# Moving the denominator and the spreads of batch 1 one slot earlier in a fused linear attention and feed-forward kernel

## The chip, the cores and the metric

One core of a Trainium2 chip. The metric is the device time of one execution in microseconds (us), as the median of several runs. The profile belongs to one further execution, and its span runs from the first to the last instruction.

## The reference

Linear attention with phi(x) = elu(x) + 1 over 8 batches, 8 heads, 576 positions and a head size of 64, then two matmuls with g = h − tanh(h) between them. The calls are cut to what matters:

```python
q_p, k_p = phi(q), phi(k)
kv  = einsum('bhsd,bhse->bhde', k_p, v)
z   = sum(k_p, axis=2)
num = einsum('bhsd,bhde->bhse', q_p, kv)
den = einsum('bhsd,bhd->bhs', q_p, z)[..., None] + 1e-6
x   = (num / den), heads put side by side      # 4608 x 512
h   = x @ w_in                                 # 512 -> 2048, "layer 1"
g   = h - tanh(h)
out = g @ w_out                                # 2048 -> 512, "layer 2"
```

## The kernel before

The 4608 rows are worked in nine chunks of 512. Layer 1 and layer 2 of a chunk are dense matmuls on TensorE. The attention for the next batch is cut into pieces that are hung between these matmuls. Layer 2 of a chunk has 16 slots of four matmuls each; `s2[n]` holds what is issued behind the four matmuls of slot n. Instructions are issued in program order on each engine, so moving a piece to another slot changes the order on several engines at once. In chunk 0, the attention of batch 1 is placed so (cut):

```python
side = Banks([4, 5, 6, 7])                 # PSUM banks, used in turn
...
s2[7].append(lambda: (a_qT_pe(1, 0, side), a_kv(1, side), a_qT_pe(1, 1, side)))
s2[8].append(lambda: b0_scale_rest(side))
s2[9].append(lambda: (a_den(1, side), num1(), a_split(1)))
s2[11].append(lambda: spread1(0))
...
s2[11].append(lambda: (exp2(qs, q_t, qp_t, "qp", 0), rest2(qs[0])))
s2[12].append(lambda: exp2(qs, q_t, qp_t, "qp", 1))
s2[13].append(lambda: (spread1(1), exp2(ks, k_t, kp_t, "kp", 0), rest2(qs[1]), a_qT_dma(2)))
s2[14].append(lambda: rest2(ks[0]))
```

- `a_qT_pe` transposes phi(q) on TensorE; ScalarE and VectorE copy the result out of PSUM (the tile `ps_all`, eight banks, which every matmul here writes).
- `a_kv` makes kv on TensorE; VectorE masks it into `kz`.
- `a_den` makes the denominator on TensorE. VectorE then adds 1e-6 and takes the reciprocal.
- `num1` makes five pieces of the numerator, which ScalarE copies to SBUF (where most other tiles lie).
- `a_split` cuts 1/den into three bf16 parts on VectorE, the last step giving `w`.
- `spread1` spreads `w` over the partitions with eight matmuls into banks 4 to 7. VectorE then multiplies two parts of the numerator by it: the "scales", which give xT, the input of layer 1 of chunk 1.
- `exp2` and `rest2` are phi of batch 2, exp on ScalarE and the rest on VectorE.
- The output blocks of layer 2 are evacuated by ScalarE at the ends of slots 12 to 15 (`evac`).

## Time and profile before

| | before |
|---|---|
| median of its first 3 runs | 293.37 us |
| span of the profiled execution | 291.8 us |
| TensorE busy | 285.5 us, 98% |
| VectorE, ScalarE busy | 175.1 us, 139.7 us |
| granted TensorE clock | 1.000 |

In the profile, PE is TensorE's matmuls, PEld its weight loads, DVE is VectorE, ACT is ScalarE. The view that counts here is the chain of work that ended last, in order of time: each piece begins where the one that released it ends. A wait of TensorE should show in it as a piece of another engine or as "issue". The lines stand in the prediction below.

### The profile page before, as it was taken

How to read it: one execution, taken by the hardware profiler on the slowest of the kernel's cores; microseconds unless marked ns; L12 is line 12 of the kernel's file. 1: busy time of each engine (PE TensorE's matmuls, PEld its weight loads, DVE VectorE, ACT ScalarE, POOL GpSimd, SP SyncE). 2: the span in 40 equal slices, each digit the busy share in tenths (PEclk: the TensorE clock that was granted, in tenths of full speed). 3: DMA queues.
4: the chain of work that ended last, by engine and by line, in shares of the span. 5: the costliest groups of instructions: out<-in, count | busy, mean ns of one | idle time of the engine just before them, and what ended most of it. 6: DMA issues, size and time to landing. Idle time of an engine off the chain costs nothing.

```text
span 291.8 us, 4505 instructions
## 1 busy us (share of the span) xinstructions
PE 285.5 (98%) x1803; PEld 134.5 (46%) x1803; DVE 175.1 (60%) x266; ACT 139.7 (48%) x168; POOL 33.7 (12%) x56
## 2 busy tenths in 40 slices
PE   8999999999999999999999999999999999999994
PEld 3544464454454444444454444444544444444443
DVE  4759958987468674776478637865581457106600
ACT  4938548846354733465345534751551155126411
POOL 8674030110030003000300030000000000000000
PEclk9999999999999999999999999999999999999999
DMA  7999999997999768965895579666117310130032
GB/s 105 193 202 212 208 206 215 194 183 149 249 158 161 175 128 137 197 146 121 136 223 123 123 139 197 146 138 139 30 38 165 73 36 0 43 83 19 0 74 72
DMA packets 39093, 38.94 MB, mean 133 GB/s; under 512 B 16352, under 2 KB 33824, under 8 KB 38304
## 3 DMA queue, kind: packets, MB, share of 16 engines
q0 software_dynamic: 17568, 18.35, 39.0%
q1 hardware_dynamic: 21344, 20.17, 30.9%
q8 instruction: 14, 0.23, 0.3%
q10 hardware_dynamic: 160, 0.13, 0.1%
q14 instruction: 7, 0.06, 0.1%
HBM read 43.91 MB, written 9.55 MB: 183 GB/s over the span
## 4 chain that ended last, share of the span: by engine, by line
PE 85%; DMA 11%; POOL 2%; issue 1%; DVE 0%; POOLq 0%
PE ps_all L387 39%; PE ps_all L366 38%; DMA v<-in_v_dram 6%; DMA w_in_sb<-in_moe_w_in_dram 3%; PE ps_all L199 2%; DMA kraw<-in_k_dram 2%; PE ps_all L317 2%; PE ps_all L618 1%; PE ps_all L276 1%; POOL v L419 1%; PE ps_all L177 1%; POOL qraw L90 0%; PE ps_all L320 0%; POOL qraw L93 0%; POOL w_out_sb L115 0%
## 5 line engine op out<-in xcount | busy, mean ns | idle before, releaser
L366 PE MATMUL ps_all<-xT,w_in_sb 128*128 128x512 bf16 x574 | 127.6, 379 | 0.0
L387 PE MATMUL ps_all<-w_out_sb,gT 128*128 128x512 bf16 x560 | 127.5, 379 | 0.0
L373 DVE TENSOR_TENSOR gT<-ps_all,th 128x1024 bf16<-128x1024 f32 x64 | 77.9, 1218 | 59.2 <-ACT th L372 59.2
L372 ACT ACTIVATE th<-ps_all 128x1024 f32<-128x1024 f32 x64 | 65.6, 1025 | 57.1 <-PE ps_all L366 46.5
L366 PEld LDWEIGHTS <-w_in_sb 128*128 128x128 bf16 x574 | 55.0, 98 | 66.1 <-issue 0.3
L387 PEld LDWEIGHTS <-gT 128*128 128x128 bf16 x560 | 54.2, 98 | 64.2
L396 ACT COPY osb<-ps_all 128x512 f32<-128x512 f32 (+1 forms) x36 | 20.9, 583 | 71.8 <-PE ps_all L387 52.6
L328 DVE TENSOR_TENSOR xT<-ps_all,rdb 128x512 bf16<-128x512 f32 x24 | 16.5, 691 | 13.7 <-PE ps_all L317 11.2
L134 ACT ACTIVATE e<-qraw 128x1152 bf16<-128x1152 bf16 x16 | 18.5, 1160 | 8.2 <-DMA qraw<-in_q_dram 8.2
L134 ACT ACTIVATE e<-kraw 128x1152 bf16<-128x1152 bf16 x15 | 17.5, 1164 | 0.3 <-DMA kraw<-in_k_dram 0.3
L136 DVE TENSOR_TENSOR qp<-e,r 128x1152 bf16<-128x1152 bf16 x16 | 12.1, 758 | 8.0 <-ACT e L134 7.2
L136 DVE TENSOR_TENSOR kp<-e,r 128x1152 bf16<-128x1152 bf16 x15 | 11.4, 759 | 7.9 <-ACT e L134 6.9
L383 POOL COPY g<-qT 1x1 bf16<-1x1 bf16 x5 | 0.9, 178 | 119.2 <-DMA qT<-qp 119.2
L378 DVE TENSOR_TENSOR gT<-ps_all,th 128x512 bf16<-128x512 f32 x16 | 10.3, 686 | 2.4 <-ACT th L377 1.7
L377 ACT ACTIVATE th<-ps_all 128x512 f32<-128x512 f32 x16 | 9.2, 598 | 4.4 <-PE ps_all L366 3.2
L447 PE MATMUL ps_all<-zero 128*128 128x512 bf16 x29 | 9.2, 480 | 1.2 <-DVE zero L405 1.2
L317 PE MATMUL ps_all<-qT,kz 128*128 128x512 bf16 x28 | 10.1, 379 | 0.0
L135 DVE TENSOR_SCALAR r<-qraw 128x1152 bf16<-128x1152 bf16 x16 | 7.3, 454 | 2.1 <-DMA qraw<-in_q_dram 2.1
L199 PEld LDWEIGHTS <-kp 64*128 64x128 bf16 x216 | 6.4, 94 | 2.5 <-issue 2.1
L285 DVE RECIPROCAL rden<-den 128x144 f32<-128x144 f32 x7 | 7.4, 1053 | 0.2
L199 PE MATMUL ps_all<-vp,kp 64*128 64x136 bf16 x216 | 7.4, 220 | 0.0
L394 DVE COPY osb<-ps_all 128x128 f32<-128x128 f32 x1 | 0.3, 292 | 11.6 <-PE ps_all L618 11.6
(85 smaller groups left out, 123.6 us busy)
## 6 DMA issues: line engine op xcount, KB each, us to landing
out_dram<-osb SPq DMA_DIRECT2D x70, 128.0 KB
rdb<-ds SPq DMA_DIRECT2D x12, 576.0 KB
kraw<-in_k_dram POOLq DMA_DIRECT2D x7, 576.0 KB, 7.1
qraw<-in_q_dram POOLq DMA_DIRECT2D x7, 576.0 KB, 9.1
v<-in_v_dram POOLq DMA_DIRECT2D x7, 576.0 KB, 11.6
w_in_sb<-in_moe_w_in_dram POOLq DMA_DIRECT2D x6, 256.0 KB, 8.7
w_out_sb<-in_moe_w_out_dram POOLq DMA_DIRECT2D x3, 512.0 KB, 14.7
qraw<-in_q_dram POOLq DMA_DIRECT2D x2, 288.0 KB, 4.4
```

The source lines that it names most:

```text
L134: return (lambda: nc.scalar.activation(e, x, AF.Exp), lambda: nc.vector.tensor_scalar(r, x, 0.0, 1.0, ALU.max, ALU.add), lambda: nc.vector ...
L136: lambda: nc.vector.tensor_tensor(y, e, r, ALU.min))
L199: nc.tensor.matmul(ps[hg][:, i, :], kp[r, i, j].rearrange("p h d -> p (h d)"), vp[r, i, j, :], start=(j == 0), stop=(j == J - 1))
L317: nc.tensor.matmul(ps, kz[:, p // 2, p % 2, 0:128], qT[:, p % 2, 0:8, p // 2, :], start=True, stop=True)
L328: nc.vector.tensor_mul(xT[:, p, S * b:S * b + 512].rearrange("p (j t c) -> p j t c", j=8, t=4), ps.rearrange("p j (t c) -> p j t c", t=4), ...
L366: nc.tensor.matmul(h, w_in_sb[:, 2 * (p % 2) + p // 2, fi * 128:(fi + 1) * 128], xT[:, p, c * 512:(c + 1) * 512], start=(n == 0), stop=(n ...
L372: nc.scalar.activation(th, h, AF.Tanh)
L373: nc.vector.tensor_sub(gT[:, fi:fi + 2, :], h, th)
L377: nc.scalar.activation(th, h, AF.Tanh)
L378: nc.vector.tensor_sub(gT[:, fi, :], h, th)
L387: nc.tensor.matmul(o, gT[:, fi, i * 128:(i + 1) * 128], w_out_sb[:, fi, :], start=(fi == 0), stop=(fi == NF - 1))
L396: nc.scalar.copy(osb[:, f0:f1], o[:, f0:f1])
```

## The change

Its intent: start 1/den and num of batch 1 one slot sooner, right behind kv and the transposes, and with it the spreads and scales, so that xT of batch 1 is complete well before layer 1 of chunk 1 needs it.

```diff
-            s2[8].append(lambda: b0_scale_rest(side))
-            s2[9].append(lambda: (a_den(1, side), num1(), a_split(1)))
-            s2[11].append(lambda: spread1(0))
+            s2[8].append(lambda: (b0_scale_rest(side), a_den(1, side), num1(), a_split(1)))
+            s2[10].append(lambda: spread1(0))
...
-            s2[11].append(lambda: (exp2(qs, q_t, qp_t, "qp", 0), rest2(qs[0])))
-            s2[12].append(lambda: exp2(qs, q_t, qp_t, "qp", 1))
-            s2[13].append(lambda: (spread1(1), exp2(ks, k_t, kp_t, "kp", 0), rest2(qs[1]), a_qT_dma(2)))
+            s2[11].append(lambda: exp2(qs, q_t, qp_t, "qp", 0))
+            s2[12].append(lambda: (spread1(1), exp2(qs, q_t, qp_t, "qp", 1), rest2(qs[0])))
+            s2[13].append(lambda: (exp2(ks, k_t, kp_t, "kp", 0), rest2(qs[1]), a_qT_dma(2)))
```

## The prediction

> **What bounds the kernel now.** I read the summary of engines first, to see whether one engine is full; then the chain of work that ended last, in order of time, to see where that engine stands still; then the timelines of VectorE and ScalarE around the moved work; and last the list of waits. The summary gives:
>
> ```profile
> PE 285.5 (98%) x1803; PEld 134.5 (46%) x1803; DVE 175.1 (60%) x266; ACT 139.7 (48%) x168; POOL 33.7 (12%) x56
> ```
>
> TensorE is busy for 98% of 291.8 us; the others have room. A busy PE need not be a PE without gaps, so the chain matters more. From 38.87 us on it lies on PE throughout, apart from slivers called "issue" and one VectorE copy at the very end. The stretch that holds the change (columns: start, length, piece) is:
>
> ```profile
> 38.87 1.66 PE ps_all L177 x36
> 40.53 0.61 PE ps_all L164 x9
> 41.14 0.86 PE ps_all L387 x4
> 42.00 0.12 PE ps_all L320 x4
> 42.12 0.86 PE ps_all L387 x4
> 42.98 0.36 PE ps_all L276 x16
> 43.35 0.22 PE ps_all L320 x4
> 43.57 0.86 PE ps_all L317 x4
> 44.43 1.73 PE ps_all L387 x8
> 46.16 0.04 issue
> 46.20 0.30 PE ps_all L354 x8
> 46.50 1.83 PE ps_all L387 x8
> 48.33 0.24 PE ps_all L354 x8
> 48.57 1.83 PE ps_all L387 x8
> 50.40 7.91 PE ps_all L366 x36
> ```
>
> Read with the program: L177 is kv of batch 1 (slot 7), L164 the second half of its transposes, each four of L387 one slot of layer 2, the first L320 the rest of batch 0 (slot 8), L276 the denominator of batch 1 and L320 with L317 its five num pieces (slot 9), L354 the two spreads (slots 11 and 13), L366 layer 1 of chunk 1. Every piece begins where the one before it ends. In these 11.5 us PE loses 0.04 us, at 46.16, in front of the first spread. The list of waits says for whom:
>
> ```profile
> PEld L354 <- DVE w L298: 0.5, 1, 0.5
> ```
>
> The weight load of the spread stood 0.5 us, waiting for the last piece of the split, but nearly all of that lies beside matmuls still running; only 0.04 us reached the chain. VectorE in the same stretch:
>
> ```profile
> 41.37 0.42 DVE L170 COPY qT<-ps_all 128x512 bf16<-128x512 bf16 x1
> 42.16 0.42 DVE L263 TENSOR_TENSOR xT<-ps_all,rdb 128x256 bf16<-128x256 f32 x1 [0.37 <-PE ps_all L320]
> 43.40 0.31 DVE L281 TENSOR_SCALAR den<-ps_all 128x144 f32<-128x144 f32 x1 [0.82 <-PE ps_all L276]
> ...
> 45.77 0.37 DVE L298 SCALAR_TENSOR_TENSOR w<-t,part,u 128x144 bf16<-128x144 bf16 x1
> 46.62 1.42 DVE L359 TENSOR_TENSOR xT<-ns,ps_all 128x576 bf16<-128x576 f32 x2 [0.48 <-PE ps_all L354]
> ```
>
> den, reciprocal and split run without a gap from 43.40 to 46.14 (45.77 + 0.37), 2.74 us. PE fills exactly this time with five num pieces and two slots of layer 2.
>
> **What the Trainium skill says.** "Perfetto Trace Analysis", section "Optimization Strategy" under "Identifying Performance Opportunities", says to find the gaps on the engine that limits and what blocks it there. The trace of before agrees that this is the question, and answers it with 0.04 us in this stretch. "TensorE: Matmul & The Clock Gate", section "Wait — 56ns, not 53.3ns?", gives 215.7 ns from start to start for 512 columns at full clock. Here 64 matmuls of layer 1 take 13.81 us, 215.8 ns each, and the granted clock is 1.000: the dense part is at its floor. "TensorEngine Tiling (Array Packing)", section "Key Properties", says a change of tiling mode drains TensorE. The trace fits: the first L320 costs 0.12 us behind dense matmuls, the same four cost 0.22 us behind the 32-column L276; and eight of L387 cost 1.83 us behind a spread against 1.73 us elsewhere. So I count the mode changes too.
>
> **The change part by part.** No instruction is added or removed, only order.
>
> 1. *The denominator, num and split go from behind slot 9 to behind slot 8.* On PE four L387 (0.86 us) change places with L276, L320 and L317 (0.36 + 0.22 + 0.86 us). PE time saved: none. The mode changes stay as many: into and out of L276, into and out of each spread. L276 now follows L320 instead of L387; its drain costs about 0.1 us in either case, I suppose.
>
> 2. *Is everything ready 0.86 us sooner?* L276 would start at 42.12. kz was written on VectorE from 40.56 for 0.89 us, until 41.45 at most; the second transposes' copies end at 41.64 (ScalarE, 40.95 + 0.69) and 41.79 (VectorE, 41.37 + 0.42). Slack 0.33 us, so no wait. The banks: num takes the banks of the two transpose copies, then that of batch 0's rest, then that of den, then the first again. Rest: VectorE frees it at 42.58 (42.16 + 0.42); PE wants it for the third piece at 42.48 + 0.22 + 0.22 = 42.92. Den: added up on VectorE by about 42.56 + 0.31 = 42.87, wanted at 43.13. The last needs ScalarE's copy of the first piece, at the same distance as before. No wait, though the margins are 0.2 to 0.3 us.
>
> 3. *The wait in front of the first spread.* Before, PE comes to it 2.81 us after the denominator's end (46.16 − 43.35). The number of slots between is still two, since the spread moves as well, so it comes at 42.48 + 2.81 = 45.29. VectorE started den 0.05 us after L276's end; now it must finish the rest's scale first (42.58), so it starts at about 42.56 (neighbours overlap a little), 0.08 us after. The split ends at 42.56 + 2.74 = 45.30, and with the 0.06 us from its end to the spread (46.14 to 46.20) the spread starts at 45.36. The wait is 0.07 us instead of 0.04: **plus 0.03 us**.
>
> 4. *The second spread.* Two slots after the first, as before. VectorE begins scaling 0.42 us after a spread starts (46.20 to 46.62) and takes 1.42 us: from 45.78 to 47.20. PE arrives at 45.36 + 0.30 + 1.83 = 47.49. No wait, margin 0.29 us as before.
>
> 5. *What follows.* xT of batch 1 was complete at 50.62 (49.21 + 1.41), while layer 1 of chunk 1 started at 50.40 and took its last part three matmuls later, at 51.05. Now it is complete at about 47.9 + 1.41 = 49.3. That is 1.3 us more slack on a wait that did not exist: **0 us**. The phi of batch 2 on VectorE is postponed behind the second scales, but that engine then has it back to back, so its end (53.09 before) moves by some 0.1 us at most. ScalarE keeps its order. Behind 50.4 us nothing on PE waits, so nothing is gained there.
>
> Sum: 0 + 0.03 + 0 = about +0.03 us on 293.37.
>
> **The rivals.** *A. The earlier scales release something.* For it: the scales ended 0.22 us after layer 1 of chunk 1 had begun, so they look late. Against: PE ran there without a gap. Gain at the most the 0.04 us, 293.33. *B. A short wait replaces the order.* With only four L387 and the rest behind the transposes, the margins of point 2 could be eaten by semaphore delays or by VectorE's copy; each missed one would cost 0.1 to 0.3 us, and since PE has no slack later nothing gives it back: 293.5 to 293.9. *C. Fewer or dearer mode changes:* L276 behind the short L320 may hide less of its weight load, or more, of the drain: 0.1 us either way. *D. A DMA:* before 38.87 the chain hangs on the load of v, which lands 16.50 us after it was issued. The change leaves all before slot 8 alone; this only brings spread from run to run.
>
> **Range and chances.** The centre is 293.4. The three runs of before span 0.38 us (293.27 to 293.65); with B and C I take 293.0 to 293.8. For 2% the time would have to move 5.9 us, more than half of the whole stretch concerned, so I give 0.985 to "within 2%", and 0.005 to faster and 0.01 to slower, as a bank wait that I misjudged can only lose.
>
> **What would show it.** Right: the chain shows, behind the rest, L276 at once, then L320 and L317, then eight of L387, a spread, eight of L387, a spread, and then twelve of L387, with a wait of 0.1 us or less before the first spread, and layer 1 of chunk 1 starting within 0.2 us of 50.40; VectorE's last scale of batch 1 ends about 1.3 us sooner, and the span is within 0.3 us. Wrong: a wait of PE at L276, L317 or a spread of 0.2 us or more (rival B), or layer 1 starting a good deal before 50.2, which would mean that PE had slack which the chain hides.

## The result, and the profile after

The changed kernel took 293.53 us in the median (293.30 to 293.99, 6 runs), the kernel before 293.60 us (293.27 to 293.74, 6 runs). The ratio is 1.000, with a 95% interval of 0.9988 to 1.0013. Ratios here are the mean time of one kernel's fast runs over that of the other's fast runs of the same rounds, so they are not quite the ratio of the medians quoted. The change is neither faster nor slower within what can be measured.

The chain of the changed kernel in the same stretch (columns: start, length, piece):

```profile
38.78 1.66 PE ps_all L177 x36
40.44 0.61 PE ps_all L164 x9
41.04 0.86 PE ps_all L387 x4
41.91 0.12 PE ps_all L320 x4
42.02 0.36 PE ps_all L276 x16
42.39 0.22 PE ps_all L320 x4
42.61 0.86 PE ps_all L317 x4
43.47 1.73 PE ps_all L387 x8
45.20 0.04 issue
45.24 0.30 PE ps_all L354 x8
45.54 1.83 PE ps_all L387 x8
47.38 0.24 PE ps_all L354 x8
47.61 2.69 PE ps_all L387 x12
50.31 7.77 PE ps_all L366 x36
```

The pieces are those of before in another order. The denominator (L276) stands directly behind the rest of batch 0 (the first L320), the spreads (L354) stand one slot sooner, and three slots of layer 2 follow the second spread instead of two. The lengths are the same to 0.01 us, the 0.04 us of "issue" before the first spread too. From 38.87 to 50.40 it took 11.53 us before; from 38.78 to 50.31 it takes 11.53 us now.

VectorE in that stretch (its timeline: start, length, engine, line, operation, operands, and in brackets the idle time before it with what ended it):

```profile
42.06 0.42 DVE L263 TENSOR_TENSOR xT<-ps_all,rdb 128x256 bf16<-128x256 f32 x1 [0.37 <-PE ps_all L320]
42.44 0.31 DVE L281 TENSOR_SCALAR den<-ps_all 128x144 f32<-128x144 f32 x1
...
44.81 0.37 DVE L298 SCALAR_TENSOR_TENSOR w<-t,part,u 128x144 bf16<-128x144 bf16 x1
45.66 1.42 DVE L359 TENSOR_TENSOR xT<-ns,ps_all 128x576 bf16<-128x576 f32 x2 [0.48 <-PE ps_all L354]
47.66 1.42 DVE L359 TENSOR_TENSOR xT<-ns,ps_all 128x576 bf16<-128x576 f32 x2 [0.58 <-PE ps_all L354]
```

The work from den to `w` takes the same 2.74 us (42.44 to 45.18), without a wait between the rest's scale and den. The last scale ends at 49.08 instead of 50.62. So xT is complete 1.23 us before layer 1 of chunk 1 begins in the chain, where before it was 0.22 us late on that scale (its last part is needed three matmuls into layer 1).

The profiled spans differ by 0.2 us (291.8 and 291.6), and the chains tell where. kv began at 38.87 before and 38.78 after: before, TensorE stood 0.22 us waiting for v. And the 36 matmuls from 50.40 on took 7.91 us before but 7.77 us after. Sixty-four such matmuls take 13.81 us elsewhere, so 36 should take 7.77: before had lost 0.14 us inside this piece. I cut that stretch into narrow windows and read the starts of the single matmuls. They are 0.216 us apart, except that in the kernel before the ninth starts 0.35 us after the eighth, at 52.10. It is the first that writes bank 2 again. That bank held the third output block of layer 2, and ScalarE's timeline has its copy out of it, merged with the next block's. First before, then after:

```profile
51.47 1.07 ACT L396 COPY osb<-ps_all 128x512 f32<-128x512 f32 x2
```

```profile
50.84 1.07 ACT L396 COPY osb<-ps_all 128x512 f32<-128x512 f32 x2
```

The first of the two copies takes 0.58 us, so before it ended at 52.05, 0.05 us ahead of that ninth matmul. In ScalarE's order it stands behind the exps of batch 2, the first of which started at 47.34 us before and at 46.71 us after, both times ended by the load of q of batch 2. Whether the change or chance moved that load was the first thing to find out.

### The profile page after: what moved, and what is told of

Read it like the earlier page. It is cut to its first block, busy times and chain, and to the rows that moved or that the text cites. A ratio compares the mean times of both kernels' runs of the same rounds, so it can differ in the third digit from the quotient of the medians.

```text
span 291.6 us, 4505 instructions
## 1 busy us (share of the span) xinstructions
PE 284.8 (98%) x1803; PEld 134.4 (46%) x1803; DVE 174.8 (60%) x266; ACT 139.6 (48%) x168; POOL 34.0 (12%) x56
## 4 chain that ended last, share of the span: by engine, by line
PE 94%; DMA 2%; POOL 1%; DVE 1%; issue 0%; DVEq 0%; POOLq 0%
PE ps_all L366 43%; PE ps_all L387 42%; DMA v<-in_v_dram 2%; PE ps_all L199 2%; PE ps_all L317 2%; PE ps_all L617 1%; PE ps_all L276 1%; PE ps_all L177 1%; PE ps_all L240 1%; POOL kraw L90 1%; DVE xT L244 0%; POOL qraw L90 0%; PE ps_all L221 0%; PE ps_all L164 0%; PE ps_all L320 0%
## 5 line engine op out<-in xcount | busy, mean ns | idle before, releaser
L317 PE MATMUL ps_all<-qT,kz 128*128 128x512 bf16 x28 | 10.1, 379 | 0.0
L447 PE MATMUL ps_all<-zero 128*128 128x512 bf16 x29 | 8.4, 448 | 1.2 <-DVE zero L405 1.2
```

The costliest lines, as they stand in the source:

```text
L317: nc.tensor.matmul(ps, kz[:, p // 2, p % 2, 0:128], qT[:, p % 2, 0:8, p // 2, :], start=True, stop=True)
```

## The experiments

For each run I read two stretches from TensorE's timeline, which give starts: **S1** from the first matmul of kv of batch 1 to the first of layer 1 of chunk 1, and **S2** from there to the first matmul of kv of batch 2. The time before S1 depends on loads; S1 starts anywhere from 38.69 to 39.21 us in the traces (v1 and v2 left out, whose block lies a slot later). What follows S2 is the same everywhere: from the first matmul of kv of batch 2 to the end of the last matmul 229.72 us pass in each of the 14 traces, by the matmuls' records. So what S1 and S2 gain or lose is neither taken up nor added to later. Without any wait inside it, S2 is 7.87 us. (q2 below is q of batch 2.)

| run | S1 us | S2 us | exp of q2 starts | median us | ratio to before, 95% interval |
|---|---|---|---|---|---|
| before | 11.37 | 8.00 | 47.34 | 293.60 | |
| changed | 11.36 | 7.87 | 46.71 | 293.53 | 1.0000 (0.9988 to 1.0013) |
| a1_after_again | 11.37 | 8.04 | 47.35 | 293.56 | 1.0006 (0.9994 to 1.0018) |
| e1_den_only | 11.27 | 8.04 | 47.10 | 293.20 | 0.9992 (0.9980 to 1.0004) |
| e1_again | 11.26 | 8.09 | 47.26 | 293.35 | 0.9997 (0.9983 to 1.0010) |
| e2_spread_only | 12.23 | 7.87 | 46.85 | 294.10 | 1.0021 (1.0008 to 1.0033) |
| e3_no_slot | 11.89 | 7.87 | 46.86 | 293.84 | 1.0012 (1.0000 to 1.0025) |
| j1_before | 11.37 | 8.54 | 47.31 | 294.21 | 1.0020 (1.0007 to 1.0034) |
| j1_after | 11.37 | 7.87 | 47.26 | 293.53 | 1.0000 (0.9987 to 1.0012) |
| v1_block_later | 10.51 | 7.86 | 47.28 | 295.07 | 1.0073 (1.0051 to 1.0094) |
| v2_exp_later | 10.50 | 7.87 | 47.40 | 295.04 | 1.0056 (1.0044 to 1.0068) |
| n1_den_exp | 11.26 | 7.87 | 46.94 | 293.31 | 0.9999 (0.9987 to 1.0012) |
| n2_after_exp | 11.36 | 8.01 | 47.62 | 293.65 | 1.0004 (0.9992 to 1.0017) |
| n3_before_exp | 11.37 | 7.91 | 47.26 | 293.39 | 1.0000 (0.9988 to 1.0013) |

All gave correct results. The kernel before was measured anew beside each group of four (medians 293.59, 293.29 and 293.44 us). Some traces miss single matmul records, which shows as one matmul fewer in a piece and a gap of 0.05 us beside it; these are not waits.

### The change again

The edit: none. Expected:

> The changed kernel again, beside the others of this group. By the traces both kernels need the same 11.53 us from kv of batch 1 to layer 1 of chunk 1, so a ratio of 1.000 with an interval that holds 1. If the change itself gains the 0.2 us by which its profiled span was shorter, the ratio is 0.9993 and the stretch is shorter than 11.53 us in this trace too. The wait of 0.13 us in layer 1 of chunk 1, seen in the first trace of before only (behind ScalarE's evacuation of the third output block, late since its exp waited for the load of q of batch 2), comes and goes with that load if it is chance.

Measured: ratio 1.0006, S1 11.37 us as before. S2 is 8.04 us here, and the delayed start is again that of the ninth matmul. The exp of q of batch 2 started late (47.35), as in the profile of before. So the 0.2 us between the first two spans were the loads of v and q in those two executions, not the change.

### Half of the change: the spreads alone

```diff
 (against the changed kernel)
-            s2[8].append(lambda: (b0_scale_rest(side), a_den(1, side), num1(), a_split(1)))
+            s2[8].append(lambda: b0_scale_rest(side))
+            s2[9].append(lambda: (a_den(1, side), num1(), a_split(1)))
```

> Only the spreads move a slot up (slots 10 and 12), the denominator stays in slot 9. My theory (TensorE has no slack from kv of batch 1 on, and the two slots of layer 2 between denominator and spread are just what VectorE's 2.7 us of den, reciprocal and split need): TensorE comes to the first spread at about 45.30 us, w is there at 46.14, so a wait of 0.90 us instead of 0.04 stands in front of the first spread, and the time is 0.86 us longer (294.2 to 294.5 beside 293.6). Rival (TensorE has slack later that takes up such a wait): a wait of 0.9 us in the chain, but the time within 0.2 us of before.

Measured: S1 12.23 us, 0.86 longer than before, as expected to the hundredth. TensorE's timeline has the wait in brackets:

```profile
46.05 0.30 PE L354 MATMUL ps_all<-w,sel 32*128 32x144 bf16 x8 [0.90 <-DVE w L298]
```

The median is 0.5 us longer than that of before in the same rounds, the interval of the ratio is worth 0.23 to 0.97 us and holds 0.86; the rival's 0.2 us lie just outside it. In the trace 0.13 us come back in S2 (7.87 instead of 8.00), since layer 1 comes too late to meet the third evacuation; behind S2 nothing takes up the rest. The distance of two slots between denominator and first spread carries the kernel, and the change kept it.

### Half of the change: the denominator alone

```diff
 (against the kernel before)
-            s2[8].append(lambda: b0_scale_rest(side))
-            s2[9].append(lambda: (a_den(1, side), num1(), a_split(1)))
+            s2[8].append(lambda: (b0_scale_rest(side), a_den(1, side), num1(), a_split(1)))
```

> Only the denominator, num and split move to slot 8, the spreads stay in slots 11 and 13. My theory: three slots instead of two lie between denominator and spread, w is ready at about 45.3 and wanted at 46.16: the wait of 0.04 us before the first spread goes, the stretch from kv to layer 1 of chunk 1 takes 11.49 us instead of 11.53, and the time is the same (0.04 us can't be seen in it). Rival (the earlier denominator gains time by itself): the stretch is shorter by 0.2 us or more.

> Only the denominator moved, once more, beside the three with the later exp. 11.27 us in the first stretch again; in the second 7.87 us if q of batch 2 lands so early that its exp starts 3.1 us or more before layer 1 of chunk 1, otherwise later by what is missing. Ratio within 0.9985 to 1.0005.

Measured: ratios 0.9992 and 0.9997, both intervals hold 1. S1 is 11.27 and 11.26 us, 0.10 us less than before, where I expected 0.04. The chain of the first of the two shows it:

```profile
43.39 2.59 PE ps_all L387 x12
45.98 0.24 PE ps_all L354 x8
```

and its timeline gives the spread itself:

```profile
45.91 0.30 PE L354 MATMUL ps_all<-w,sel 32*128 32x144 bf16 x8
```

Nothing stands between the three slots and the spread. The spread is not shorter, it takes 0.30 us in both kernels, but without the wait it starts 0.07 us ahead of the recorded end of the matmuls before it (45.91 against 45.98), and with the wait 0.04 us behind that end (46.20 against 46.16). So the wait had cost 0.10 us, of which the chain shows 0.04 us as a gap.

In both runs S2 lost 0.17 to 0.22 us to the third evacuation. The loss can be worked out: in all four traces that show it alone (before, a1, e1 and its repeat) the time from the start of the exp of q2 to the start of layer 1, plus the loss in S2, is 3.04 us (before: 2.90 + 0.14), and j1_after below, with 3.10 us, loses nothing. The repeat's expectation had put this limit at 3.1. So for the same late landing of q2, a TensorE that comes 0.10 us sooner in S1 gives those 0.10 us back in S2. In the second run the chain itself runs through that load:

```profile
38.64 8.54 DMA qraw<-in_q_dram
...
47.26 1.16 ACT e L134
...
51.49 0.48 ACT osb L396
51.98 0.04 issue
52.02 4.26 PE ps_all L366 x19
```

It reads: the load of q of batch 2 lands, ScalarE's exp starts, the evacuation (osb) follows behind the exps, and the ninth matmul of layer 1 follows 0.04 us behind that.

### One slot further than the change

```diff
 (against the changed kernel)
-            s2[7].append(lambda: (a_qT_pe(1, 0, side), a_kv(1, side), a_qT_pe(1, 1, side)))
-            s2[8].append(lambda: (b0_scale_rest(side), a_den(1, side), num1(), a_split(1)))
-            s2[10].append(lambda: spread1(0))
+            s2[7].append(lambda: (a_qT_pe(1, 0, side), a_kv(1, side), a_qT_pe(1, 1, side),
+                                  b0_scale_rest(side), a_den(1, side), num1(), a_split(1)))
+            s2[9].append(lambda: spread1(0))
...
-            s2[12].append(lambda: (spread1(1), exp2(...), rest2(qs[0])))
+            s2[11].append(lambda: spread1(1))
+            s2[12].append(lambda: (exp2(...), rest2(qs[0])))
```

> The whole block one slot further up than in the change: rest, denominator, num and split in slot 7 right behind the second transposes, spreads in slots 9 and 11. My theory: the denominator now has to wait for VectorE's and ScalarE's copies of those transposes and for kz, which end 0.65 us behind the transposes; the rest covers 0.12 us, so TensorE stands about 0.45 us before or within the denominator, and the time is 0.45 us longer than before (294.0). Rival B of the prediction, taken further (bank waits add up): also waits of 0.1 to 0.3 us before the num pieces, 0.6 us or more in all. Rival that nothing waits: within 0.1 us.

Measured: S1 11.89 us, 0.52 us longer, and 0.35 us by the ratio (interval 0 to 0.73 us). The chain leaves TensorE for the masking of kz:

```profile
40.91 0.89 DVE kz L186 x2
41.80 0.04 issue
41.84 0.31 PE ps_all L276 x8
```

The denominator could start 0.04 us after kz was ready, not sooner. Its second half waited shortly for the transposes' copy, and no bank wait followed before the num pieces. So one slot of dense work between transposes and denominator is needed, and one is enough: rival B of the prediction exists, but begins only past the change.

### What the change bought: a delay put in on purpose

```diff
 (against each of the two kernels)
             def spread1(h):
                 sub["bp"] = a_spread_pe(1, 4, (2 * h, 2 * h + 1))
+                if h:
+                    nc.vector.reciprocal(junk, junk)      # 128x144 f32 scratch of ones, 1.05 us
```

> Kernel before with one more reciprocal of 1.05 us on VectorE (on a scratch tile) ahead of the scales of the second spread. Theory that the change bought slack, not time: here the last two parts of xT come 1.05 us later, at about 50.97 and 51.67, while layer 1 of chunk 1 wants them at 50.67 and 50.88: TensorE waits about 0.85 us there, and the time is 0.85 us longer (294.4). Rival (the end of the scales is far from limiting in both kernels): 0 to 0.1 us.

> The changed kernel with the same additional reciprocal of 1.05 us at the same place. Theory that the change bought slack: the scales end at about 49.5 instead of 49.1, still before layer 1 of chunk 1 needs them at 50.8, so TensorE waits at most 0.1 us (for VectorE's second subtraction of chunk 1, which comes some 0.4 us later) and the time is within 0.1 us of the changed kernel. Rival (both kernels are alike in this): as much as the kernel before with the same addition.

Measured: the kernel before loses, the changed kernel does not. Before, with the delay, VectorE's second scales and then TensorE's layer 1 of chunk 1 (a matmul record is missing within the latter):

```profile
50.27 1.35 DVE L360 TENSOR_TENSOR xT<-ns,ps_all 128x576 bf16<-128x576 f32 x2
```

```profile
51.67 7.28 PE L367 MATMUL ps_all<-xT,w_in_sb 128*128 128x512 bf16 x32 [0.28 <-DVE xT L360]
```

The third matmul of layer 1 waited 0.23 us and the fourth 0.44 us for their parts of xT, 0.67 us in all; S2 is 8.54 instead of 7.87. I had expected 0.85 us: the whole trace stands 0.11 us later than that of before, while the scales ended at 51.62, 0.05 us sooner than I had put them without that shift, so the wait is smaller. The time is 1.0020 of before (0.2 to 1.0 us). The changed kernel with the same delay has its scales done at 49.53 us, 0.8 us ahead of layer 1, S2 at 7.87 us and a ratio of 1.0000. So the change bought slack in front of layer 1 of chunk 1, about 1.4 us (from 0.22 us late to 1.23 us early in the chains above), which the kernel before did not lack.

### An attempt to use it: the whole block later

```diff
 (against the kernel before)
-            s2[7].append(lambda: (a_qT_pe(1, 0, side), a_kv(1, side), a_qT_pe(1, 1, side)))
-            s2[8].append(lambda: b0_scale_rest(side))
-            s2[9].append(lambda: (a_den(1, side), num1(), a_split(1)))
+            s2[8].append(lambda: (a_qT_pe(1, 0, side), a_kv(1, side), a_qT_pe(1, 1, side)))
+            s2[9].append(lambda: (b0_scale_rest(side), a_den(1, side), num1(), a_split(1)))
```

> Since one slot between the transposes and the denominator was enough, move the other end: transposes and kv of batch 1 to slot 8, rest, denominator, num and split in slot 9, spreads in 11 and 13 as before. Theory: in the first trace of before TensorE stood 0.28 us in front of kv for the load of v, in that of after 0.01 us; a slot later (0.86 us) the load has always landed, so this wait is 0 and the gain over before is 0 to 0.3 us (ratio 0.9990 to 1.000), by how late the load is. Rival: the block comes too close to the spreads or to layer 1 of chunk 1 and waits 0.1 us or more there.

> As the one with the block later, and the exp of the first half of k of batch 2 on ScalarE behind the evacuation of slot 14 instead of that of slot 13. Theory: the evacuation of the third output block then comes about 1.1 us sooner and the wait of 0.13 us for it in layer 1 of chunk 1 can't appear; a gain over before of 0.1 to 0.4 us (ratio 0.9987 to 0.9997). Rival: the fourth evacuation, now behind that exp, becomes the late one, and TensorE waits for its bank three matmul groups into chunk 1.

(v2 has, besides, the exp of k of batch 2 in slot 14 instead of 13; its diff is shown in the next part.) Measured: both miss, and are 1.6 to 2.1 us slower, clear of the noise. TensorE's timeline of v1 has the reason in brackets:

```profile
39.77 1.02 PE L387 MATMUL ps_all<-w_out_sb,gT 128*128 128x512 bf16 x4 [1.55 <-DMA w_out_sb<-in_moe_w_out_dram]
```

Slot 8 is the first that reads the third quarter of w_out, and this had only landed when slot 8 already wanted it. In the kernel before, kv and the transposes stand in front of slot 8 and cover that load (it lands at 40.09 there, and slot 8 starts at 41.14). I had looked at the load of v alone. S1 is short in these two runs only because the block lies behind one slot more. What v2 was to test could not be seen in it.

### The evacuation of the third block

```diff
 (against e1_den_only, and likewise against before; the changed kernel has no spread1(1) here)
-            s2[13].append(lambda: (spread1(1), exp2(ks, k_t, kp_t, "kp", 0), rest2(qs[1]), a_qT_dma(2)))
-            s2[14].append(lambda: rest2(ks[0]))
+            s2[13].append(lambda: (spread1(1), rest2(qs[1]), a_qT_dma(2)))
+            s2[14].append(lambda: (exp2(ks, k_t, kp_t, "kp", 0), rest2(ks[0])))
```

> The version with only the denominator moved, and the exp of k of batch 2 behind the evacuation of slot 14. From the traces so far: the stretch from the start of kv to the start of layer 1 of chunk 1 takes 11.27 us (11.37 before, since no wait stands before the first spread), and from there to kv of batch 2 7.87 us whatever the time at which q of batch 2 lands (8.00 and 8.04 us where the third evacuation came late). So 0.1 to 0.3 us faster than before, ratio 0.9990 to 0.9997; the interval will hardly exclude 1. Rival: the fourth evacuation is late instead, and the second stretch stays above 7.95 us.

> The changed kernel with the exp of k of batch 2 behind the evacuation of slot 14. Theory: 11.37 and 7.87 us in the two stretches, also where q of batch 2 lands late (its exp starting at 47.3 us or later); ratio 0.9993 to 1.0. Rival: the wait in layer 1 of chunk 1 has another cause than the third evacuation, and 8.0 us appear again with a late q.

> The kernel before with the exp of k of batch 2 behind the evacuation of slot 14. Theory: 11.37 and 7.87 us in the two stretches, as in the changed kernel with the same edit, since the wait of 0.13 us was ScalarE's and not VectorE's; ratio 0.9993 to 1.0. Rival: it was VectorE's (the later scales and phi), then 8.0 us stay here and are gone only in the changed kernel.

Measured: in none of the three does the ninth matmul of layer 1 start late any more. In n2 and n3 q2 landed so late that by the 3.04 us above it would have waited 0.29 and 0.19 us, so that wait was ScalarE's evacuation; in n1 the exp started 3.03 us ahead of layer 1, where less than 0.01 us would have been lost anyway, so n1 shows nothing of this. But n2 loses 0.14 us and n3 0.04 us at another place, the first matmul of the ninth group, which writes bank 2 once more. In n2, where q2 landed latest of all, it started at 57.42, behind this subtraction, the second of chunk 1:

```profile
56.15 1.22 DVE L373 TENSOR_TENSOR gT<-ps_all,th 128x1024 bf16<-128x1024 f32 x1
```

which ends at 57.37 (in n3 57.06 behind 57.01). The fourth evacuation now stands behind the exp, and the tanh and subtractions behind it. So the expectation failed in n2, and its rival (another cause) is right in part: the late load of q2 finds a second way to TensorE. In n1 both stretches are free of waits, 11.26 and 7.87 us, 0.24 us less than the 19.37 us of before. Yet its median is only 0.13 us below that of before in the same rounds, and the ratio 0.9999 does not show it: the start of S1 alone differs more from run to run. I found no version that measurably beats both kernels.

## Why the prediction was right

The time was foretold as 293.4 us in 293.0 to 293.8, and 293.53 us was measured, "same" as given with 0.985. The number alone proves little, since six runs of one kernel span 0.5 to 0.7 us and would also fit a change of ±0.1 us; what bears the mechanism out is S1, the same to 0.01 us.

- **Point 1, only the order changes on TensorE: right.** S1 is 11.36 us after 11.37. The supposition that the denominator's mode change costs the same behind the short L320 was right too, 0.36 us both times, and it starts 0.07 us ahead of the recorded end of the piece before it in both kernels; so rival C did not come about.
- **Point 2, everything is ready 0.86 us sooner: right.** No wait stands before L276, L320 or L317. The slot further up (e3) shows how near its edge is: there 0.5 us are lost to kz and the copies.
- **Point 3, plus 0.03 us before the first spread: wrong by that 0.03.** den started 0.05 us after the denominator's end, as before, since VectorE began it 0.04 us ahead of the rest's recorded end. The gap stayed at 0.04 us. Also, rival A's ceiling of 0.04 us was too low: e1 shows that the wait cost 0.10 us, as the spread can start ahead of the recorded end of the matmuls before it.
- **Point 4, no wait before the second spread: right.** The scales ended at 47.08 and the spread began at 47.38 in the chain, 0.30 us apart, predicted 0.29.
- **Point 5, xT's greater slack is worth nothing: right, and tested** with the added delay, which costs the kernel before 0.67 us in front of layer 1 and the changed kernel nothing. The last scale came 1.54 us sooner, of which 0.09 us are the whole trace's shift; I had said 1.3, having counted 0.42 us from the spread's place in the chain to its scales, where 0.28 us passed (47.38 to 47.66). The phi of batch 2 on VectorE ended at 52.78 instead of 53.09, 0.2 us sooner by the same account, where I had allowed 0.1.
- **The sentence "Behind 50.4 us nothing on PE waits" was wrong.** The line I quoted for it, 7.91 us for 36 matmuls, held a wait of 0.14 us: it should have been divided by its count. The wait comes from the load of q of batch 2 through ScalarE's order, appears in both kernels (S2 of a1 is 8.04 us), and so did not spoil the sum. That was luck in part: two traces of the changed kernel differ by 0.17 us in S2, which the range took in without naming this load.
- **Rival D, loads that land at different times,** is what the difference of the two profiled spans came from: 0.09 us at kv and 0.14 us at the third evacuation.

## What to carry to other kernels

Here the limiting engine already ran almost without gaps across the stretch, and moving its pieces about changed slack and not time; ask first which wait would end sooner, and divide each merged piece by its count, since waits hide in it (0.14 us in 36 matmuls here). Keep the distance between a producer on one engine and its consumer on another when moving both, and before moving a block away from a place, ask which load it had been covering there: kv and the transposes, moved one slot down, uncovered a load of w_out and cost 1.6 to 2.1 us, more than anything else tried.

## What the Trainium skill lacked or had wrong

- "TensorEngine Tiling (Array Packing)", section "Key Properties", says that a change of tiling mode drains TensorE, but not what it costs. Here a matmul started 0.16 us ahead of the recorded end of the one before it where both were of the 128x128 form, but only 0.07 us ahead where the form changed, to fewer rows or columns and back alike: about 0.10 us for each change. In the chain this is 0.22 against 0.12 us for the same four matmuls behind 32-column ones, and 1.83 against 1.73 us for eight dense ones behind a spread. Whether the drain is all of it was not tested.
- No page that I read says how far a matmul may start ahead of the recorded end of one in another tiling mode. Because of those 0.07 us, a visible gap of 0.04 us before a spread stood for a wait of 0.10 us (S1 11.37 us with it, 11.27 without).
- "Perfetto Trace Analysis", section "Per-instruction lifecycle: what the profiler-reported window actually captures", puts semaphore propagation outside the windows and gives no figure there. From the end of `w` on VectorE to the spread on TensorE it was 0.06 us in the chain's terms (45.18 to 45.24), the start of the spread's weight load included, and 0.04 us from kz to the denominator in e3.
